# Attention and a gated network on one core: another table of pages and banks for the same work

## The chip, the core and the metric

The kernel runs on one NeuronCore of a Trainium2 chip. Its engines are named as in the profile: PE multiplies matrices (PEld loads its weights), DVE, ACT and POOL work on vectors, SP issues nearly all transfers (DMAs). The metric is the device time of one execution in microseconds (us); the time of a kernel is the median of several executions.

## The reference

Attention over 8 batches and 8 heads: 32 global positions look at everything, 512 local positions look at the global ones and at a window of 32 to each side. The result goes through a normalisation and a gated network.

```python
s_g = scale * np.matmul(q_g, k_all.transpose(0, 1, 3, 2))
out_g = np.matmul(sm(s_g), v_all)
...
s_l = np.concatenate([s_lg, s_ll], axis=-1)
out_l = np.matmul(sm(s_l), np.concatenate([v_g, v_l], axis=2))
...
xn = x / rms * rms_g
g = xn @ w_gate
silu = g * (1.0 / (1.0 + np.exp(-g)))
val = xn @ w_val
return (silu * val @ w_out)
```

There are 4608 tokens of 512 features, and 1536 hidden features.

## The kernel before

The tokens are worked through in chunks: chunks 0 to 7 are the 512 local positions of one batch each, chunk 8 holds the global positions of all. A step has a name of a chunk, a colon, a letter with numbers and a count. In a chunk, `P` are the matrix products of the network, `R` what ACT, DVE and POOL do with their results (`R45.0` computes the tanh `t11`), `t` the tail of a gated product, `w` loads and stores. `L`, `S`, `T`, `A`, `B`, `Y` and others are the attention of the next chunk, laid between them: loads of queries and keys, scores, transposes, products with values. Weights for later chunks are brought to a form of two float16 pieces once, stored to memory (`wd`, `wa`, `wb`) and loaded again as `wt` (input side) and `wu` (output side).

Nothing is scheduled by a planner at run time or by priorities: the table `ORDER` names the steps in one written order, which sets the order on every engine and in SP's queue. An instruction starts when its engine has come to it and the data and the memory that it uses are free.

All larger temporaries lie in 43 pages of 1024 float32 per partition (1152 for the 8 pages called wide, `W0` to `W7` or `w0` to `w7`), and products in 8 banks. Two more tables say where: `PAGES` has one entry for each temporary in the order in which they are asked for (1198; `13a` is page 13 from its first quarter, `41c` page 41 from its third), `BANKS` one for each product (438). `tile_of` and `bank_of` read the next entry. A temporary that is given a page waits until the last reader of the one before is done; where that reader is a transfer, until it has landed.

Some pages are neighbours in memory, in chains given by `CHAINS`; `link` holds each pair of neighbours as one piece of 2048 (two times 1024). `convert(i)` brings weight tile i (0 to 11 are `w_in`, 12 to 17 `w_out`) to its form. `load` asks for two pages; if they are neighbours, the steps behind it (rebias `m`, third piece `k`, sign `g`) work on both halves in one 1024-wide instruction, otherwise in two 512-wide ones.

Names that come up below: `t11` of step `1:R45.0`, `po2` of `1:P60.0`, `p0_11` read by `1:R45` and `1:R46`, `wq6` read by the store `1:w23.0`; `t4` of `2:R20.0`, `o1` read by the store `1:R59.1`; the loads `gv10` (`2:GL/1+1.0`), `q60` to `k61` (`1:L/0+2.0`), `wt3_21` (`3:w6.0`), `wt2_13` (`1:w49.1`), `wt2_40` (`2:w18.0`) and the temporary `s6_0` (chunk 2).

Of the kernel before, what the change touches and what calls it, by code (L numbers as in the profile page):

```python
# [62 lines left out]
NPAGE, NWIDE = 43, 8  # L63

CHAINS = (
    (7, 8, 22, 25), (9, 10), (12, 11, 18), (13, 40), (14, 4, 27, 23, 39), (15, 26), (16, 17),
    (28, 29), (30, 31), (32, 33), (34, 35), (41, 42),
)

ORDER = """  # L70
# [324 lines left out]
"""  # L395

PAGES = """
0a 0c 1a 0c 1a 5a 6a 0c 1a 11a 12a 13a 4a 2a 3a 1c 14a 15a 2a 5a 2c 4a 11a 2c 5c 7a 8a 3a 16a 17a
18a 19a 2a 20a 21a 6a 22a 8a 1a 2a 9a 10a 6a 1a 11a 18a 17a 16a 21a 1c 12a 9a 24a 1a 20a 7a 13a 0c
5c 6c 6d 0d 5d 20a 15a 23a 20b 3a 11a 10a 23a 27a 14a 4a 2a 22a 25a 28a 29a W7a 3a 11c 14a 8a 17c  # L400
27a 32a 34a 18a 19a 20c 19a 1a 6a 30a 31a 3a 7a 26a 15a 13a 40a 16a 1c 42a 34a 35a 22a 38a 2a 28a
15a 26a W2a 15c 14a 30a 41a 42a 7a 41a 7a 25a 4a 9c 38a 32a 33a 18a 29a 41c 4a 27a 23a 39a 5a 4c 24a
20c 31a 17a 33a 4c 4c 40a 4c 42a 2c 3a 9c 6a 18a 28a 11a 41c 27a 1a 9a 33a 0c 20a 18a 7a 40a 33a 36a
37a 38a W0a W1a 17a 24a 0a 2a 2a 28c 28c W3a W4a W5a W4c W6a 23a 39a 31a 3c 27a 31c 3a 0a 36a 31d 3b
2a 2b 13a 31a 31b 27c w6 w4 42a 15a 27a 2c 37c 24a 24a 41c 28a 34a 24c 41a 9a 9a 33a 27a w1 w0 5a
36a 37c 37c 13a 18a 2c 12a w0 32a 37a 23a 23a 18a 23c 21a 7a 15a 4a 19a 17c 8a 3c W6a 41c 39a 8a 36a
w2 w5 34a 17a 34c 37a 23c 3c 42a 33a 21a 27a 18a 23a 8a 4a 13a 32a 41a W7a 34a 21a 10a 0a 26a 0a 15a
22a 0a 34c 28a W5a 27c 34c 23a w7 w6 10a 13a 25a 39a 41a 39a 12c 25a 39c 41c 30a 41c 25b 37d 29a 37a
12d 37c 25c 24a 24b 23c 12a 18a 30a 13a w1 w4 35a 8a 15a 39c 4a 17a 9a 13c 41a 25c 18a 0a w4 26a W7a
19a 16a 32a 2a 22a W2a 13a 27a 3a 5a 3c 33a 19a 16a 37a 28c 21a 8a 26a 41a 0a 17a 34a 22a 5a W6a 3a  # L410
9a W0a 28a w2 w6 41c 8c 14a 28a 13a 27a 33a 2a 17a 8a 21a 5a 34a 4a 39a 13a 41c W7a 39a 3a 9a W5a
12a 36a 3a W1a 18a 33a 8a 37a 30a 21a 0a 41a 35a 34a 14a 5a 9a 32a 35a 12a 33a 41c 29a 13a 8c 29a 9a
w6 w1 13c 10a 13c 13a 14c 29a 41a 13a 22b 13c 14a 11c 17a 11a 22c 22d 29c 20a 41a 22a 13d 34a 14c
14d 4a 13a 26a 30a 31a 32a 14a w6 w2 3a 29a 0a 9a 39a 34a 37a 33a 36a 4a 42a w2 15a 40a 14a 34a 7a
31a 9a 25a 8a 28a 8c 21a 3a 15a 9a 35a 10a 42a 31a 37a 0a 11a 31c 31a 39a 34a 26a W7a 31a 36a w2 w7
34a 38a 7a 28a 21a 24a 25a 25c 1a 31c 8a 24a 12a 8a 13a 25a 19a 11a 1a 5a 7c 39c 38a 30a 26a 24a 41a
38a 10a W1a 33a 22a 27a 29c W6a 40c 35a 22c 13a 37a 5a 27a 10a 12a 26a 15a 35a 13a 24a 34a 35c 30a
3a 23a 5c 39c w2 w1 35a 18a 5a 29a 39a 4a 37a 14c 41a 5a 22a 22b W2a 5c 22c 34a 26a 23a W5a 38a 38d
29c 34a 23a 5c 38b 22c 9a 6a 38c 14c 42a 41a 24a W0a 16a 10a 42a w7 w6 40a 2a 6a 42c 26a 4a 15a 17a
32a 3a w1 8a 30c 42c 42a 29a 5a 16a 7a 14a 21a 30a 1a 39a 4a 21a 2a 39a 5a 1c 24a 16a 20a 4a 16a 37a  # L420
17a 4a W2a 14a 29a w1 w2 7a 6a 42a 26a 2a 19a 17c 17a 9a 1a 16a 20a 36a 17a 14a 9a 37a 15a 23a 25a
30a 30c 30a 31a 3a 7a 1a 37a 25a 5a 36a 31a W7a 24a 3a 24c W1a 42a 22a 0a 30a 6a 32a 39a 20a 4a 7a
30a 9a 40a 7c 1a 39a 35a 14c 7a w0 w5 7a W6a 7c 36a 14a W0a 24a 7a 12a 20c 12a 12b 19a 20c 7c 3a 35a
14a 13a 12d 30a 20a 10a W5a 7a 30c 30d 39a W4a 12c 30b 28a 23a W6a 26a 25a 32a 26a w7 w4 37a 8a 20a
15c 3a 40a 6a 28a 7a 15a w6 41a 13a 26c 20a 33a 25a 4a 1a 13c 29a 24a 21a 36a 17a 39a 25a 18a 4a 15a
20a 21a 16a 15a 26c 42a 40a 8a 31a 15a 29a w6 w5 33a 5a 24a 2a 23a W5a 1c 1a 38a 26c 28a 16a W7a 14a
3a 42a W0a 8a 33a 0a 13c 28c 28a W1a 4a 5a 9a 38a 13a 27a 26a 17a 22a 3c W4a 25a 31a 4a 4c 18a 20a
16a 37a 0a 34a 24a 30c 5a 36a 40a 12a 4a 22a W2a 3a 12a w2 w0 12c 35a 3a 15a 12a 0a 18a 34c 10a 22a
14c 14d 19a 34a 22c 25a 40a 8a 8a 14a 14b 3c 39a W2a 29a 15a 22c 24a 28a 15b 22d 4a 10a 26a W6a 41a
41a 3c w0 w1 9a 42a 12a 19a 28a 19a 4a 35a 29a 33a w1 20a 15c 12a 12c 34a 3a 37a 23a 22a 5a 38a 24a  # L430
25a 35a 12a 42a 2a 35a 19a 28a 33a 0a 3a 15c 26a 9a 37a 40a 3a 34a w3 w7 9a 21a 15c 20a 23a 18a 19c
37a 7a 38a 24a 0a 16a 3a 22a 26a 27a 18a 21a W7a 38c 3a 19c 6a 40a 24a 1a 20a 4a W2a 16a 6a W4a 15c
19c W0a 7a 0a 31a 24a 19c 25a 14a 11a 19a 35a 0a 42a 7c 7a 19c 28a 33a 7a W3a 9a 13a 33c 33a 33b 30a
30c 19a 42a 20a W7a 30c 25a 6a W1a 33c 30a 30b 35a 10a 30d 25b 32a 13a 15a W4a 36a 5a w1 w6 29a 19a
10a 31a 32a 40a 15a 14a w6 19c 19a 37a 34a 17c 36a 7a 22a 19a 31a 27a 5a 13a 2a 10a 24a 36a 36c 24a
41a 14a 17a 36a 17c 37a 21a 7a 14a W4a w2 w0 39a 22a 22c 27a 2a 34a 26a 22a 38a 8a 41a 21a W5a w6
42a 33c 24c 17a 9a 7a 12a 2a W4a 27a W3a 32a 23a 41a 20a 38a 12a 33a 12a W5a 32a 23a 23a 12a 2a W0a
15a 24a 40a 33a 17a 4a 17a 1a 6a 23c 23a 23a 15a 3a 23a 16a 33a 32a 14a 25a W6a 39a 24a 34a W5a 14a
21c 21d 11a 18a 14c 31a 8a 13a 6a W7a 20a 20b 28a 16a 20c 14c 14d 0a 21a 21b 37a 18a 30a 39a 0a 8a
9a 31a 26a 39a 28c 32a 29a 37a 7a 25a 32a W3a 30a 34a 5a 28a 20c 3a 10a 28a 27a 28a 3a W2a 24a 39a  # L440
2a 39c 14a 37a 36a 0a 42a 18a 11a 23a 9a 0a 19a 21c 29a 7a 1a 22a 29a 35a 26a 5a 23a W1a 14a 29c 38a
13a 27a 40a 27a 10a 41a 2a 12a 4a 13c 13a 15a 13a 42a 17a 31a 16a 40a
"""

BANKS = """
# [9 lines left out]
"""  # L455


# [1915 lines left out]
```

## Time and profile before

| | us |
|---|---|
| median of 3 runs | 900.91 (900.81 to 901.15) |
| profiled execution | 902.12 |
| its span, first to last instruction | 900.3 |
| PE busy | 867.6 (96%) |
| DVE busy | 709.8 (79%) |
| ACT busy | 556.1 (62%) |
| POOL busy | 278.1 (31%) |
| mean granted clock of PE | 0.989 |

The rows come from one profiled execution, 1.2 us above the median. Times in the rows count from the start of the span. Nearly every instruction is issued by one helper, so the rows have one line, L2132; they are told apart by time, tile and shape. In them `chain` is a page of a chain, `page` a single page, `wide` a wide one, `bank` a product.

### The profile page before, as it was taken

The page shows a single profiled execution, that of the slowest core. Times are in us where ns is not written, and L with a number is a line of the kernel's source. Part 1 is how long each engine was busy: PE and PEld are TensorE (multiplying, and loading weights), DVE is VectorE, ACT ScalarE, POOL GpSimd, SP SyncE. Part 2 cuts the span into 40 slices and gives each one's busy share as a digit, 9 for nine tenths or more (in the row PEclk, how much of TensorE's full clock was granted, in tenths as well). Part 3 has the DMA queues.
Part 4 walks back from the last instruction along what each step waited for, and adds up shares of the span by engine and source line. Part 5 has one row for each costly group of instructions (what it writes and reads, how often), then busy time and mean ns, then how long its engine had stood idle before and what let it go on. Part 6 is the DMA issues. An engine that isn't in the chain of part 4 may idle for free. (4 is left out here: it accounts for less than half of the span.)

```text
span 900.3 us, 28280 instructions
## 1 busy us (share of the span) xinstructions
PE 867.6 (96%) x11646; PEld 669.2 (74%) x11646; DVE 709.8 (79%) x1822; ACT 556.1 (62%) x1337; POOL 278.1 (31%) x255
## 2 busy tenths in 40 slices
PE   4799999999799899999999999999999999999998
PEld 3655456454448786588888888888888888888997
DVE  5999999888485666867876799788886888587576
ACT  6999993646334563647574775658575773545443
POOL 0000000125624467403641245214440345134414
PEclk9799999999899999999999999999999999999999
DMA  9997300688957676994799277777697579736571
GB/s 353 404 388 313 126 1 2 187 282 283 373 190 222 202 242 218 317 325 149 257 337 331 97 244 250 269 260 264 208 389 268 188 235 354 260 106 207 215 268 48
DMA packets 102737, 216.79 MB, mean 241 GB/s; under 512 B 8272, under 2 KB 34640, under 8 KB 102608
## 3 DMA queue, kind: packets, MB, share of 16 engines
q1 hardware_dynamic: 102176, 214.66, 68.8%
q8 instruction: 91, 1.49, 0.7%
q10 hardware_dynamic: 432, 0.33, 0.1%
q14 instruction: 38, 0.31, 0.1%
HBM read 187.96 MB, written 27.00 MB: 239 GB/s over the span
## 5 line engine op out<-in xcount | busy, mean ns | idle before, releaser
L2132 PEld LDWEIGHTS <-chain 128*128 128x128 f16 (+1 forms) x3744 | 346.3, 98 | 128.4 <-issue 12.9
L2132 PE MATMUL bank<-chain,chain 128*128 128x256 f16 (+6 forms) x3061 | 298.4, 270 | 5.0 <-ACT chain L2132 3.6
L2132 PE MATMUL bank<-page,chain 64*32 64x128 f32 (+5 forms) x1857 | 222.9, 298 | 1.2 <-ACT chain L2132 0.4
L2132 PEld LDWEIGHTS <-page 128*128 128x128 f16 x1704 | 160.7, 98 | 47.5 <-issue 7.8
L2132 POOL TENSOR_TENSOR chain<-chain,chain 128x512 f16<-128x512 f32 (+4 forms) x95 | 104.8, 1113 | 168.3 <-ACT chain L2132 128.3
L2132 PE MATMUL bank<-chain,page 128*128 128x256 f16 (+7 forms) x1377 | 151.8, 273 | 0.1
L2132 PE MATMUL bank<-page,page 64*32 64x128 f32 (+6 forms) x1231 | 105.0, 293 | 16.1 <-DMA page<-in_qk_dram 5.9
L2132 ACT COPY chain<-bank 128x512 f32<-128x512 f32 (+3 forms) x125 | 64.1, 531 | 79.2 <-PE bank L2132 66.5
L2132 DVE TENSOR_TENSOR chain<-bank,chain 128x512 f32<-128x512 f32 (+1 forms) x106 | 67.4, 645 | 48.5 <-PE bank L2132 32.6
L2132 ACT CAST chain<-chain 128x512 f16<-128x512 f32 (+2 forms) x87 | 66.5, 776 | 46.9 <-DVE chain L2132 36.7
L2132 ACT ACTIVATE chain<-chain,sm 128x128 f32<-128x128 f32 x200 | 74.2, 391 | 23.4 <-DVE sm L2132 23.0
L2132 POOL TENSOR_TENSOR page<-chain,page 128x512 f16<-128x512 f32 (+1 forms) x45 | 49.4, 1109 | 73.0 <-ACT page L2132 52.9
L2132 PE MATMUL bank<-wide,chain 32*64 32x96 f32 (+6 forms) x1834 | 65.5, 264 | 0.7 <-issue 0.7
L2132 ACT COPY page<-bank 128x512 f32<-128x512 f32 (+3 forms) x64 | 32.7, 519 | 44.0 <-PE bank L2132 38.8
L2132 DVE TENSOR_TENSOR chain<-chain,chain 128x256 f32<-128x256 f32 (+5 forms) x91 | 56.3, 628 | 4.6 <-ACT chain L2132 3.7
L2132 PEld LDWEIGHTS <-wide 128*128 128x128 f16 x570 | 52.9, 99 | 9.3 <-DMA wb<-chain 0.2
L2132 ACT ACTIVATE page<-page,sm 128x128 f32<-128x128 f32 x152 | 56.0, 391 | 4.4 <-DVE sm L2132 4.1
L2132 POOL TENSOR_TENSOR chain<-page,chain 128x512 f16<-128x512 f32 (+3 forms) x33 | 37.6, 1144 | 68.1 <-ACT chain L2132 64.3
L2132 POOL TENSOR_TENSOR page<-page,sm 128x512 f32<-128x512 f32 x3 | 4.1, 1368 | 176.2 <-DVE sm L2132 176.2
L2132 ACT ACTIVATE chain<-chain 128x512 f32<-128x512 f32 (+3 forms) x39 | 49.7, 1294 | 2.6 <-DVE chain L2132 1.5
L2132 PE MATMUL bank<-chain,wide 128*128 128x256 f16 (+1 forms) x392 | 48.6, 271 | 0.0
L2132 DVE CUSTOM_DVE_ANT_0 chain<-bank,wide 128x128 f32<-128x128 f32 x136 | 34.8, 283 | 12.5 <-PE bank L2132 10.1
(229 smaller groups left out, 1316.5 us busy)
## 6 DMA issues: line engine op xcount, KB each, us to landing
chain<-wd SPq DMA_DIRECT2D x77, 512.0 KB, 7.3
page<-wd SPq DMA_DIRECT2D x33, 512.0 KB, 7.6
chain<-in_w_in_dram SPq DMA_DIRECT2D x24, 512.0 KB, 9.0
chain<-wb SPq DMA_DIRECT2D x19, 512.0 KB, 7.7
wide<-in_gkq_dram SPq DMA_DIRECT2D x16, 576.0 KB, 6.6
wide<-wd SPq DMA_DIRECT2D x16, 512.0 KB, 7.9
chain<-wa SPq DMA_DIRECT2D x14, 512.0 KB, 6.6
chain<-in_vb_dram SPq DMA_DIRECT2D x18, 352.0 KB, 5.7
```

Of the source, the lines that this page charges most:

```text
L2132: return lambda *a, **k: write(self.engine, lambda: call(*a, **k))
```

## The change

The three tables are replaced: other chains, 1150 of the 1198 entries of `PAGES`, and 387 of the 438 of `BANKS`. `ORDER`, the number of pages and banks, and all code stay. The loads that asked for neighbouring pages find other neighbours: before, the two pages of all eighteen weight tiles were neighbours, now of sixteen.

```diff
 CHAINS = (
-    (7, 8, 22, 25), (9, 10), (12, 11, 18), (13, 40), (14, 4, 27, 23, 39), (15, 26), (16, 17),
-    (28, 29), (30, 31), (32, 33), (34, 35), (41, 42),
+    (1, 21), (2, 3), (6, 22), (8, 27, 30, 15, 14, 11, 12), (9, 35), (16, 17), (25, 26, 28),
+    (31, 32), (33, 34), (40, 41),
 )
...
 PAGES = """
-0a 0c 1a 0c 1a 5a 6a 0c 1a 11a 12a 13a 4a 2a 3a 1c 14a 15a 2a 5a 2c 4a 11a 2c 5c 7a 8a 3a 16a 17a
...
+0a 0c 1a 2a 2c 7a 8a 2c 9c 16a 17a 6a 10a 3a 4a 3c 18a 19a 5a 10a 5c 6a 7a 9a 7c 11a 12a 13a 20a 21a
...
 BANKS = """
-0 1 6 7 5 1 2 3 4 5 7 6 2 0 2 3 2 7 5 3 4 3 0 2 5 0 2 0 4 7 2 7 6 4 5 3 0 2 3 7 3 6 7 1 6 1 3 2 6 0
...
+0 1 6 7 1 5 2 3 4 1 7 2 6 0 2 3 2 7 3 3 4 1 0 6 4 0 6 0 3 7 6 7 2 3 4 1 0 1 1 7 6 2 7 5 0 5 2 1 3 6
...
```

The entries of the temporaries named above, read off by counting:

| temporary | before | after |
|---|---|---|
| `t11` of `1:R45.0` | 13a | 34c |
| `wq6` (store `1:w23.0`) | 13a | 18a |
| `p0_11`, `po2` | bank 4, bank 4 | bank 3, bank 7 |
| `t4` of `2:R20.0` | 41c | 15a |
| `o1` (store `1:R59.1`) | 41c | 38c |

## Rows read from the trace of the kernel before

**Rows 1.** The page's first part: busy time, share and instructions of each engine.

```profile
PE 867.6 (96%) x11646; PEld 669.2 (74%) x11646; DVE 709.8 (79%) x1822; ACT 556.1 (62%) x1337; POOL 278.1 (31%) x255
```

**Rows 2.** The waits of PE: who was waited for, total us, times, longest.

```profile
PE bank L2132 <- ACT chain L2132: 8.7, 5, 4.7
...
PE bank L2132 <- DVE chain L2132: 5.7, 5, 4.5
```

**Rows 3.** PE's timeline: start, us, operation; idle time before it and its releaser in brackets.

```profile
103.01 0.59 PE L2132 MATMUL bank<-page,chain 128*128 128x512 f16 x2 [0.27 <-DVE chain L2132]
...
111.80 0.81 PE L2132 MATMUL bank<-page,chain 128*128 128x512 f16 x3 [0.43 <-ACT chain L2132]
...
241.99 2.72 PE L2132 MATMUL bank<-page,page 128*128 128x512 f16 x6 [4.53 <-DVE chain L2132]
244.64 0.44 PE L2132 MATMUL bank<-wide,chain 64*32 64x128 f32 x4
...
295.90 1.36 PE L2132 MATMUL bank<-chain,wide 128*128 128x256 f16 x11
...
313.88 0.27 PE L2132 MATMUL bank<-chain,chain 128*128 128x256 f16 x1 [2.87 <-ACT chain L2132]
```

**Rows 4.** ACT's timeline at the two stalls.

```profile
234.49 0.35 ACT L2132 COPY page<-bank 128x256 f32<-128x256 f32 x1
...
240.53 0.69 ACT L2132 ACTIVATE chain<-bank,half_inv 128x512 f32<-128x512 f32 x1 [5.02 <-DMA wd<-chain]
...
312.64 0.72 ACT L2132 ACTIVATE chain<-page,half_inv 128x512 f32<-128x512 f32 x1 [3.56 <-DMA out_dram<-chain]
313.27 0.57 ACT L2132 COPY chain<-bank 128x512 f32<-128x512 f32 x1
```

**Rows 5.** DVE's timeline at the first stall.

```profile
241.25 0.69 DVE L2132 SCALAR_TENSOR_TENSOR chain<-chain,bank 128x512 f32<-128x512 f32 x1 [7.06 <-ACT chain L2132]
```

**Rows 6.** SP's timeline: when transfers were issued; a merged row includes waits between.

```profile
204.02 11.69 SPq L2132 DMA_DIRECT2D wd<-chain  x3
...
224.58 0.33 SPq L2132 DMA_DIRECT2D page<-in_qkb_dram  x1
...
278.38 1.25 SPq L2132 DMA_DIRECT2D wide<-wd  x2
...
284.10 0.37 SPq L2132 DMA_DIRECT2D chain<-wd  x1
...
304.77 0.46 SPq L2132 DMA_DIRECT2D out_dram<-chain  x1
```

**Rows 7.** Narrow windows: length, busy us of five engines, PE's clock, DMA share, GB/s.

```profile
242.00:246.70 4.70, 4.70 (x86) 2.77 (x93) 2.91 (x4) 0.62 (x1) 2.45 (x2) 0.50 1.05 382
...
315.00:318.40 3.40, 3.40 (x19) 2.42 (x17) 1.58 (x3) 2.75 (x11) 1.79 (x2) 0.50 1.11 379
440.00:450.00 10.00, 8.80 (x325) 7.45 (x322) 7.98 (x21) 6.07 (x9) 4.93 (x5) 1.00 0.99 385
```

**Rows 8.** Groups by shape: count, busy us, mean ns of one, idle before.

```profile
L2132 ACT CAST chain<-chain 128x1024 f16<-128x1024 f32 x34 | 35.2, 1041 | 21.1 <-DVE chain L2132 12.1 <-DVE sm L2132 5.8 <-issue 2.7
L2132 ACT CAST chain<-chain 128x512 f16<-128x512 f32 x51 | 30.7, 614 | 16.5 <-DVE chain L2132 15.4 <-PE bank L2132 0.7 <-DMA out_dram<-chain 0.2
...
L2132 DVE SCALAR_TENSOR_TENSOR chain<-chain,chain 128x512 f32<-128x512 f32 x38 | 29.2, 779 | 8.8 <-ACT chain L2132 8.8
...
L2132 DVE SCALAR_TENSOR_TENSOR chain<-chain,bank 128x512 f32<-128x512 f32 x18 | 12.1, 679 | 7.5 <-ACT chain L2132 7.5
...
L2132 DVE SCALAR_TENSOR_TENSOR chain<-chain,ends,chain 128x1024 int32<-128x1024 int32 x8 | 10.2, 1274 | 1.1 <-ACT chain L2132 1.0
```

**Rows 9.** The window of the conversions, columns as in group 7.

```profile
75.00:100.00 25.00, 24.98 (x206) 12.21 (x204) 24.71 (x56) 24.97 (x40) 0.00 (x0) 1.00 0.45 168
```

**Rows 10.** The page's DMA issues: count, KB each, median us from issue to landing.

```profile
wide<-wd SPq DMA_DIRECT2D x16, 512.0 KB, 7.9
...
chain<-in_qkb_dram SPq DMA_DIRECT2D x15, 256.0 KB, 8.3
```

More of the change, by code (lines that the diff above doesn't have):

```diff
@@ L397 @@
 PAGES = """
-0a 0c 1a 0c 1a 5a 6a 0c 1a 11a 12a 13a 4a 2a 3a 1c 14a 15a 2a 5a 2c 4a 11a 2c 5c 7a 8a 3a 16a 17a
[L399 to L442, printed above, removed]
+0a 0c 1a 2a 2c 7a 8a 2c 9c 16a 17a 6a 10a 3a 4a 3c 18a 19a 5a 10a 5c 6a 7a 9a 7c 11a 12a 13a 20a 21a
@@ new lines @@
+22a 1a 2c 23a 24a 3a 25a 26a 5a 2c 14a 15a 7a 12a 14a 11a 2a 3a 19a 18a 17a 12a 29a 18a 16a 4a 10a
+16c 23a 24c 24d 16d 23b 23c 9c 28a 23d 7a 14a 13a 15a 30a 8a 27a 20a 21a 1a 31a 32a W7a W1a 14c 4a
+25a 18c 27a W2a 26a 11a 5a 12c 5a 2a 16a 33a 34a 36a 8a 6a 22a 42a W0a 3a 2c 30a 26a 28a 31a 24a 20a
+10a 22a 6a 21a 22c 4a 33a W1a W2a 8a 35a 8a 1a 9a 0c 39a 35a 9a 11a 32a 24a 27a 30a 40a 41a 24a 9c
+29a 12c 34a 18a 36a 9c 9c 35c 9c 30a 20c 36a 0c 16a 11a 10a 39a 12c 27a 2a 12a 14a 35c 21a 11a 8a
@@ new lines @@
+23a 14a 37a 38a 24a 15a 7a 18a 29a 35a 37a 20a 10c 10c W3a W4a W5a W4c W6a 40a 41a 34a 35c 37a 34c
+35a 7a 20a 34d 35b 34a 34b 42c 27a 27b 37c w6 w4 30a 22a 29c 27c 38a 15a 36a 38c 10a 15a 29a 42a 7a
+12a 14a 36a w2 w1 0a 20a 36a 38a 18a W1a 27c 30a w1 26a 36c 36a 19a 5a 19c 40a 22a 28a 9a 29a 17a
+25a 17c W6a 38c 41a 25a 14a w7 w5 12a 37a 35c 36a 12c 17c 42c 11a 13a 38a 13a 9a 6a W0a 34c 17a 12a
+25a 19c 26a 10a 14a 40a 15a W7a 26a 14a 12c 8a W0a 34a 37c 28c w5 w6 11a 31a 38a 28c 37c 18a 30c 38a
@@ new lines @@
+28c 38c 35a 38c 38b 32d 13a 32a 30d 32c 19c 18c 18d 20a 30a 31a 35a 36a w2 w4 29a 41a 40a 1c 4a 0a
+10a 30a 37c 30a W5a 17a w2 11a 4a 3a 19a W6a 27a 26a W1a 36a 1a 37a 22a 28a 33a 22a 10a 32a 28a 25a
+17a 11a 37c 15a 0a 34a 26a 10a 41a 5a 22a 5a 18a w2 w1 15a 15c 7a 18a 4a 6a W2a 27a 0a 37a 35a 6a
+25a 8a 1a 38c 15a W7a 6a 17a 27a 34a 19c 19a 17a W4a 33a 35a 32a 1c 5a 8a W0a 37c 3a 11a 25a 38a 7a
+35a 3a 27a 6a 18a 35a 18c 30c 7a 17a w0 w6 7c 9a 7a 18c 16a 18a 38a 16c 26d 7a 11a 26a 0a 18c 16c
@@ new lines @@
+16d 7c 21a 37c 26c 16a 25a 26a 26b 14a 23a 29a 19a 12a 1a 12c w0 w1 27a 40a 30a 17a 25c 37a 1a 6a
+15a 14a 42a w1 W2a 40c 7c 17a 31a 37a 12a 34a 10a 32a 10c 20a 27a 42a 15a 24a 25a 42a 7c 30a 38a 13a
+12a 7c W7a 33a 23a 3a 37a 2a w7 w4 33a 18a 37c 31a 20a W4a 32c 25a 19a 12a 10a 13a 8a 19a 37a 30a
+28a 6a 13a 5a 32a 32c 25a 11a 23a 18a 9a 18a 10a 14a 3a 16a 41a W6a W0a W6c W1a 40c 16c 34a 7a 27a
+42a 8a 23a 12a 26c 28a W4a 37a 23a 11a 33a 17a 25a 26a w7 w6 23c 29a 40c 26c 25a 24a 34a 7a W6a 13c
@@ new lines @@
+13a 13b W7a 26a 28a 8a 37a 21a 35a 18a 18d 7c 8a 21a 1a 18b 28a 34a 39a 18c 28c 32a 24a 3a 36a 22a
+39a 26a w0 w1 30a 4a 40a 15a 37a 33a 1a 0a 25a 15a w6 35a 26c 26a 13c 19a 22a 32a W2a 11a 20a 11c
+16a W2a 40a 16a 36a 40a 22a 28b 3a 19a 10a 33a 15c W4a 0a 20a W7a 26c 32a w0 w4 34a 12a 26a 37a 20a
+9a 10a 15c W0a 11c 19a 0a 2a 10a 11a 36a W7a 1a 21a 41a 13c 13a 13c 5a 33a 11a 22a 13a 41a 35a 2a 5a
+W1a W7a W0a W7c W4a 26a 15c 38a 33a 12a 25a 40a 0a 11a 3a 33a 36a 30a 15a 3a 40a 29a 26a 15c w6 w7
@@ new lines @@
+15c 4a 15a 36a 38a W6a 26a 15c 14a 15a 36c 36d 9a 8c 36a 0a 3a 27a 7a 8d 38a 8a 39a 27a 38c 8a 8b
+40a W5a 8c 38b 31a 21a W0a 29a 20a 25a 38c w1 w5 33a 34a 15a 34c 0a W4a 15a 31a 12a 19a w0 7a 32a
+29a 36a 6a 11a 20a 1a 32c 24a 3a 16a 13a 10a 29a 11a 23a 21a 34a 0a 3a 2a 34a 36a 28a 19a 40a W7a
+34a 9a w7 w6 6a 35a 32c 24a 31a W6a 23a 16c 18a 36a 20a 1a W5a 27a 16a 28a W1a 2a 6a 30a 14a 35a 16c
+4a 33a 20a 41a 7a 14a 42a 32a 10a 22a 23c 40a W4a 11a 36a 38c W0a 33a 21a 35a 20a 37a 30a 8a 36a 13a
@@ new lines @@
+19a 38c 4a 22a W2a 23a 33a w6 w2 38a 26a 33a 34a 23a 39a 11a 37c W6a 6a 27c 27d 5a 37a 6c 40a 19a 2a
+2a 27a 27b 33c 29a W2a 9a 34a 6c 16a 16a 34b 6d 4a 10a 32a W0a 18a 18a 16a w1 w5 W7a W1a 23a 34c 25a
+28a 4a 26a 9a 39a w5 8a 34c 6a 21a 36a 33a 35a 31a 7a W6a 7c W2a 21a 28a 23a 25a 24a 26a 16c 37a 33a
+5a 6a 8a 32a 40a 35a 19a 6a 36a w3 w6 40a 3a 16c 8a 31a 11a 26a 5c 12a W2a 7a W6a W0a 0a 26c 32a 20a
+35a 3a 0a 5a 26a 5c 15a 19a 11a 1a 26a 4a 2a 16a 15a 42a 27c 6a W1a 12a 8a 38a 11a 6a 21a 27a 17a
@@ new lines @@
+42a 28a 6a 25a 42c 6c 42c 37a 33a 8a W0a 40a 14a 15c 15a 15b 41a 41c 42a 35a 0a W3a 41c 21a 33a 38a
+15c 41a 41b 28a 7a 41d 21b 30a 14a 29a W6a 13a 39a w7 w5 9a 42a 38a 12a 13a W2a 11a 27a w5 42a 15c
+10a W7a 29a 30a 8a 1a 14a 12a 5a 39a 42a 24a 38a 24a 15c 30a 26a 7a 27a 22a 8a 9a 10a 3a 28a 27a W2a
+w1 w7 2a 15c 24a 5a 1a 29a 32a 26a 20a 19a 7a 3a W4a w5 35a 21c 15c 24c 40a 28a 4a 1a W2a W4a W0a
+13a 31a 7a 0a 20a 4a 24c 4a 15a 13a 31a 2a 19a 1a W1a 11a 24a 30a 21a 9c 23a 9a 34a 33a 21a 21c 21c
@@ L443 @@
+11a 36a 21c 16a 2a 31a 27a 4a W5a 13a 34a 29a W7a 27c 27a 27b 17a 25a 27a 39a 28a 42a 24a W6a 0a 0b
+37a 16a 0c 3c 27c 6a 3a 3b 5a 37a 41a 8a 6a 31a 40a 39a 10a 34a 29a 31a 15a 5a 32a 14a 25a W0a 41a
+37a 12a 28c 0c 33a 38a 25a 14a 5a 13a 22a 4a 42a 1a 8a 28a 26a 20a 29a 35a 8a 10a 11a 40a 29a 21a
+27a 12c 17a 36a 34a 33a 18a 28a 41a 19a W3a 12a 15a 23a 32a 33a W1a 15a 6a W4a 1a 11a 7a 12a 12c 30a
+35a 12a 9a 39a 32a 13a
 """
 BANKS = """
[9 rows of a table removed]
[9 rows of a table added]
 """
```

16 rows, old and new, of the table BANKS are left out of this document.

## Prediction

> **What bounds the kernel now.** I read the page's busy table first: PE is busy 867.6 us of a span of 900.3, 96% [rows 1], so only PE's idle time and its clock can give anything back; a faster engine beside it gives nothing. The list of what PE waited for comes second [rows 2]: 8.7 us for ACT in five waits, the longest 4.7, and 5.7 us for DVE in five, the longest 4.5. The reader is to see that this is a handful of stalls, not many small ones. PE's timeline then places them. Those of the first 50 us follow loads and data, which the change leaves alone. Two lie later: 4.53 us before 241.99, behind DVE, and 2.87 us before 313.88, behind ACT [rows 3].
>
> The third reading is what held those engines. ACT's timeline shows, at 240.53, an activation that had waited 5.02 us for a DMA that reads a page into `wd`, and at 312.64 one that had waited 3.56 us for a DMA into the output [rows 4]. DVE's instruction at 241.25 waited 7.06 us for the first of these [rows 5], and PE for DVE. So the causes of both PE stalls are pages: a temporary was given a page that a slow store was still reading. By the tables, `t11` (step `1:R45.0`) shares page 13 with `wq6`, which store `1:w23.0` reads; the product `po2` (step `1:P60.0`) shares bank 4 with `p0_11`, which waits to be read by `R45` and `R46`. `t4` (step `2:R20.0`) shares page 41 with `o1`, which store `1:R59.1` reads. The second store was issued at 304.77 [rows 6], 7.9 us before its ACT instruction began, which is about as long as a transfer takes here [rows 10]; the first lies in the same way.
>
> The fourth reading is the clock. [...] Behind two short idle times within 440 to 450 us it stays 1.00 [rows 7]. [...]
>
> **The change part by part.** No operation, no DMA and no order is altered, only the page and the bank of each temporary.
>
> *First stall.* In the new tables `t11` has page 34, which no store reads late, and `po2` has bank 7, which ACT empties with the copies that end at 234.84 [rows 4]. ACT had been idle since 240.53 - 5.02 = 235.51 [rows 4] with its input there, and PE's work before the stall ended at 241.99 - 4.53 = 237.46 [rows 3]. `P60` needs neither `R45` nor `R46` for its data, so it follows at once: 4.53 us. Half of the 4.70 us at the half clock [rows 7] goes too, since the same columns take half the time: 2.35 us. Together 6.9 us. What is late next is a chain over POOL and DVE whose result PE wants some 8 us later; followed step by step on the old times it moves with PE but for some 0.2 us, so I keep 6.7.
>
> *Second stall.* `t4` moves to page 15, which DVE has released by then. ACT, idle since 312.64 - 3.56 = 309.08, runs `t4` there (0.72), and the copy that PE waits for (0.57) follows by 310.4 [rows 4]; PE's earlier work ends at 313.88 - 2.87 = 311.01 [rows 3]. The cover is 0.6 us. Gain 2.87 + 3.40/2 = 4.57 us. What is late next is weight tile `wt2_40`, issued right behind the store of 304.77 [rows 6] and first used 4 us behind the stall, some 4.2 us after its landing; the gain eats that margin, and I put 0.2 us against it: 4.4 kept.
>
> *Small bank waits.* One of 0.27 us at 103.01 [rows 3] and one more of 0.2 come from a shared bank that is no longer shared; I count 0.3 as gain. The 0.43 us at 111.80 [rows 3] are data and stay.
>
> *What is added, first: split conversions.* A weight whose two halves lie on neighbouring pages of one chain is converted in 1024-wide instructions. By the tables all eighteen were so before; now tiles 12 and 14 (`w_out` 0 and 2) are not. "Sixteen joined" is thus two fewer, and costs six instructions: two on ACT, four on DVE. ACT: 2 x 0.614 - 1.041 = 0.19 us each; DVE: 2 x 0.679 - 1.274 = 0.08, or 2 x 0.779 - 1.274 = 0.28, each [rows 8]. That makes 0.37 us on ACT and 0.3 to 1.1 on DVE. They run between 85 and 115 us, where ACT is busy 24.97 and DVE 24.71 of 25 us [rows 9], so no cover is there but PE's own lead; PE has three short waits behind these engines. Ends 0 and 1.5; I take 0.4, nearest to the ACT row, since the wait at 111.80 is behind ACT. [...]
>
> *What is added, second: holds of the DMA queue.* SP issues all these transfers in the written order; one whose page is not yet free holds all behind it. The new tables let freed pages rest longer before ACT, DVE or POOL reuse them (least time between a store's landing and a compute instruction on its page: 5.5 us instead of under 0.1), and pay with loads that take pages sooner. I laid the new pages on the old times. The worst hold is 12.2 us (`gv10`, from 202.9), in a stretch where the queue stood 11.7 us inside three stores anyway [rows 6]. What hangs on it is loads up to that at 224.58 [rows 6], some 2 to 3 us later, so from 226.6, landing 8.3 us after issue [rows 10] at 234.9; they are first used at 244.64 [rows 3], 238.8 once the stall is gone: 3.9 us left. The next: the load issued at 278.38 is held until `s6_0` is released at 284.10, as the next load was before [rows 6]; plus 7.9 us [rows 10] is 292.0, against first use at 295.90 [rows 3]: 3.9 left. Three more, at 287, 518 and 716 us, keep 5 to 6.5. Every load still lands in time: cost 0, with ends 0 and some 14 (the slower rival). PE's start may lose 0.3 by an ACT instruction there that now shares a page with a later reader, and the end of the program 0.1.
>
> *The sum*, against the profiled execution's own 902.12 us: 902.12 - 6.7 - 4.4 - 0.3 + 0.4 + 0.3 + 0.1 = 891.5. The median of the runs shown is 1.2 us below the profiled execution, so the median to come is 890.3.
>
> **The rivals.**
> (a) Half of it is kept. The chain POOL, DVE, PE behind 250 us, or a load, takes the first stall's place; then 6.7 us stay lost: 897.0. Or the second stays: 894.7. For it: DVE waits for POOL at several places between 245 and 265. Against it: POOL's work there follows results of PE and ACT that move too.
> (b) The change does not do what it says: both waits find another late reader, and the time stays at 901. Against it: the new pages of `t11` and `t4` were free 4 us and more before these two began, by the tables on the old times.
> (c) Slower: the holds of SP's queue outgrow the margins. Transfers pile up behind a hold and start together when it ends, so each could land later than its row says. If five places with 3.9, 3.9, 4.7, 5.9 and 6.5 us left are each held 7.0 us more, PE loses 3.1 + 3.1 + 2.3 + 1.1 + 0.5 = 10.1, and behind the two longest the half clock costs 2.35 + 1.70 again [rows 7]: 14.2 us, so 904.5. The point from which it decides is about 6.3 us more at each, where some 6.7 + 4.05 eat the whole gain of 10.6. Against it: 7.0 us is nearly a whole transfer's 7.9 [rows 10].
> (d) The clock. The new banks could make PE pause shortly and often, and the clock fall between: each fall at the price of rows 7, about 2 us; one or two of these give 892 to 894.5. The short pauses of the old run left it at 1.00 [rows 7]. [...]
>
> **How the numbers follow.** Forecast 0.70; (a) 0.14; (b) 0.05; (c) 0.08; (d) 0.03. The forecast's own range is 888.5 (splits free, no follower) to 892 (splits at their upper end, wt2_40 late). The range to hold 8 in 10 goes on through (d) and (a) to 897.5, and a little below for slack that I do not see: 887.5 to 897.5. Faster by over 0.2% (1.8 us, about what a measurement of this kernel can tell from no change): 0.70 + 0.14 + 0.02 and no more, 0.86; within 0.2%: 0.06; slower: 0.08.
>
> **What would show it.** Right, if in the new profile PE has no stall over 1 us after 50 us, the clock is 1.00 from 225 to 320, and ACT's waits for `wd<-chain` and `out_dram<-chain` are gone; the splits show as six more instructions between 85 and 115, and PE's waits there grow by under 1 us. Wrong in (a): a new PE wait near 238 or 250, or 311. Wrong in (c): PE or its weight loads wait for a DMA `chain<-wd` or `chain<-in_qkb`, above all near 239, 290, 297, 525 and 725, with SP waiting just before. What would make the whole wrong is a transfer that lands far later than its row of the old run, since all margins are laid on old times.

## The result and the profile after

| | before | after |
|---|---|---|
| median, us | 900.86 (900.05 to 901.15, 4 runs) | 889.75 (888.94 to 890.10, 4 runs) |
| profiled execution, its span | 902.12, 900.3 | 889.73, 887.9 |
| PE busy, mean granted clock | 867.6, 0.989 | 862.6, 0.991 |

The ratio is 0.9877, 95% interval 0.986 to 0.9894: 11.1 us faster by the medians, and 12.4 us between the two profiled executions (902.12 and 889.73). The forecast said 890.3.

The list of PE's waits after the change (who was waited for, total us, times, longest us), against [rows 2]:

```profile
PE bank L2133 <- DMA chain<-in_qk_dram: 5.7, 1, 5.7
PE bank L2133 <- DVE chain L2133: 5.3, 3, 4.9
PE bank L2133 <- ACT chain L2133: 5.0, 1, 5.0
PE bank L2133 <- ACT page L2133: 1.8, 3, 1.2
...
PE bank L2133 <- DVE sm L2133: 0.8, 1, 0.8
```

Three long waits are left, 5.7, 4.9 and 5.0, all in the first 40 us. The 4.53 and the 2.87 us of [rows 3] are gone, and a wait of 0.8 behind DVE's `sm` is new. The windows of the two stalls and of the short pauses (length, busy us of PE, PEld, DVE, ACT, POOL, granted clock, DMA share, GB/s), against [rows 7]:

```profile
225.00:250.00 25.00, 24.96 (x458) 13.59 (x457) 17.97 (x59) 10.07 (x28) 16.33 (x13) 1.00 1.06 370
300.00:325.00 25.00, 25.00 (x293) 21.61 (x292) 21.42 (x56) 19.62 (x58) 16.10 (x12) 1.00 0.85 293
440.00:450.00 10.00, 10.00 (x92) 8.72 (x91) 7.27 (x20) 5.20 (x12) 5.92 (x6) 1.00 1.01 318
```

PE is busy for all but 0.04 us of the 25 us in each of the first two, and the granted clock is 1.00. In the timelines (start, us, operation, idle time in brackets) the places of [rows 3] and [rows 4] now read, first PE's:

```profile
237.99 1.70 PE L2133 MATMUL bank<-chain,chain 128*128 128x512 f16 x10
...
304.60 1.47 PE L2133 MATMUL bank<-chain,chain 128*128 128x256 f16 x12
```

ACT's timeline of the same kernel:

```profile
236.13 0.67 ACT L2133 ACTIVATE chain<-bank,half_inv 128x512 f32<-128x512 f32 x1
...
302.66 0.72 ACT L2133 ACTIVATE chain<-page,half_inv 128x512 f32<-128x512 f32 x1
303.54 0.59 ACT L2133 COPY chain<-bank 128x512 f32<-128x512 f32 x1 [0.16 <-PE bank L2133]
```

`P60`, at 237.99, and `P25`, which now runs within the row at 304.60, follow the work before them without a pause; `t11` (236.13) and `t4` (302.66) begin as soon as ACT comes to them.

Lining up every product of PE in the two traces gives the time by place: the start of the same product, after minus before (a negative number is time gained by then).

| at (us, before) | after minus before, us | what lies between |
|---|---|---|
| 43 | +0.79 | start |
| 213 | -0.18 | conversions, short bank waits |
| 236 | +0.69 | the new wait of 0.83 before `1:P30.0` |
| 250 | -6.26 | first stall and its slow clock: -6.95 |
| 300 | -6.25 | |
| 320 | -10.95 | second stall and its slow clock: -4.70 |
| 450 | -11.91 | short waits |
| 890 | -12.38 | short waits |

### The profile page after: what moved, and what is told of

Its sections match the earlier page's. It is cut to its first block, busy times and chain, and to the rows that moved or that the text cites. A ratio compares the mean times of both kernels' runs of the same rounds, so it can differ in the third digit from the quotient of the medians.

```text
span 887.9 us, 28263 instructions
## 1 busy us (share of the span) xinstructions
PE 862.6 (97%) x11646; PEld 666.8 (75%) x11646; DVE 710.8 (80%) x1826; ACT 555.6 (63%) x1339; POOL 279.1 (31%) x255
## 4 chain that ended last, share of the span: by engine, by line
PE 84%; DVE 5%; ACT 2%; issue 1%; DMA 1%; POOL 0%; SPq 0%; POOLq 0%; ACTq 0%
PE bank L2133 84%; DVE chain L2133 3%; DVE page L2133 2%; ACT chain L2133 1%; DMA wide<-in_gkq_dram 1%; ACT page L2133 1%; DVE wide L2133 0%; POOL chain L2133 0%; SPq L2133 0%; POOL page L2133 0%; DVE nt L2133 0%; DVE xg L2133 0%; DVE sm L2133 0%; DVE hs L2133 0%; ACT sm L2133 0%
## 5 line engine op out<-in xcount | busy, mean ns | idle before, releaser
L2133 PEld LDWEIGHTS <-chain 128*128 128x128 f16 (+1 forms) x3369 | 309.9, 98 | 105.2 <-issue 7.8
L2133 PE MATMUL bank<-chain,chain 128*128 128x256 f16 (+5 forms) x2406 | 263.0, 277 | 1.7 <-DVE sm L2133 0.8
L2133 PE MATMUL bank<-page,chain 128*128 128x256 f16 (+6 forms) x1689 | 203.3, 289 | 0.9 <-DMA page<-in_qk_dram 0.6
L2133 PE MATMUL bank<-chain,page 128*128 128x256 f16 (+6 forms) x1887 | 181.9, 286 | 11.9 <-DMA chain<-in_qk_dram 5.7
L2133 PE MATMUL bank<-page,page 128*128 128x256 f16 (+5 forms) x1171 | 119.7, 277 | 1.7 <-ACT page L2133 1.4
L2133 POOL TENSOR_TENSOR chain<-chain,chain 128x512 f16<-128x512 f32 (+5 forms) x66 | 73.8, 1125 | 131.8 <-ACT chain L2133 95.4
L2133 POOL TENSOR_TENSOR page<-chain,page 128x512 f16<-128x512 f32 (+3 forms) x50 | 56.8, 1147 | 97.5 <-ACT page L2133 97.3
L2133 PE MATMUL bank<-chain,wide 128*128 128x256 f16 (+3 forms) x482 | 61.5, 278 | 0.1
L2133 ACT COPY page<-bank 128x512 f32<-128x512 f32 (+2 forms) x73 | 38.3, 541 | 35.5 <-PE bank L2133 31.8
L2133 ACT CAST page<-chain 128x512 f16<-128x512 f32 (+2 forms) x42 | 33.9, 813 | 34.9 <-DVE chain L2133 28.2
L2133 POOL TENSOR_TENSOR chain<-page,chain 128x512 f16<-128x512 f32 (+3 forms) x34 | 38.9, 1150 | 52.5 <-ACT chain L2133 52.5
```

The costliest lines, as they stand in the source:

```text
L2133: return lambda *a, **k: write(self.engine, lambda: call(*a, **k))
```

## The experiments

The kernel before and the changed kernel were run again beside them; before had medians of 899.5 to 900.6 and the changed kernel 889.58 (888.15 to 890.27). Each run is compared by its ratio to the kernel before on its own chip; the ratios stand with their 95% intervals in brackets and are not exactly the quotients of the medians. Entries of a table are counted from 0.

> The changed kernel itself, beside the next two on one chip: 889.7 by every theory.

It measured 889.58, ratio 0.9883 (0.9864 to 0.9901).

### One entry: t11

Entry 263 of `PAGES`, the third of these five:

```diff
-8a 4a 13a 32a 41a
+8a 4a 16c 32a 41a
```

> The kernel before with one entry of the page table changed: t11 of step 1:R45.0 goes from page 13 (still read by the store of wq6) to the third quarter of page 16, which nobody has used for long. Theory (one shared page is the whole first stall): PE's wait of 4.53 us before 1:P60.0 and the half clock behind it go, 6.7 to 7.1 us, so 893.8 to 894.2. Rival (the next wait in the chain over POOL and DVE takes its place): 1 to 4 us gained, 897 to 900. Rival (the wait belongs to the bank that po2 shares, so the page alone does nothing): 900.9.

Measured: 903.83 against 899.51, ratio 1.0037 (1.0019 to 1.0056): slower. PE's row of this run:

```profile
251.05 0.61 PE L2132 MATMUL bank<-nt,same 128*128 128x16 f32 x2 [7.12 <-DVE sm L2132]
```

DVE's row:

```profile
249.47 0.29 DVE L2132 CUSTOM_DVE_ANT_0 chain<-bank,wide 128x128 f32<-128x128 f32 x1 [6.76 <-DMA wd<-chain]
```

Two of its windows, columns as above:

```profile
246.00:251.00 5.00, 0.00 (x0) 0.00 (x0) 1.45 (x13) 0.39 (x2) 0.00 (x0) 0.68 1.08 381
251.00:255.00 4.00, 3.95 (x12) 1.73 (x13) 3.74 (x17) 1.50 (x9) 0.00 (x0) 0.54 1.06 355
```

The same place in the kernel before, first DVE's rows:

```profile
248.68 0.29 DVE L2132 CUSTOM_DVE_ANT_0 chain<-bank,wide 128x128 f32<-128x128 f32 x1 [1.67 <-DMA wd<-chain]
...
249.22 0.29 DVE L2132 CUSTOM_DVE_ANT_0 chain<-bank,wide 128x128 f32<-128x128 f32 x1 [0.24 <-DMA wd<-chain]
```

And PE's row there, with no wait before it:

```profile
250.42 0.39 PE L2132 MATMUL bank<-nt,same 128*128 128x16 f32 x2
```

The wait before `P60` is gone, PE comes to `1:n55.0` 6.5 us earlier (251.05 - 7.12 = 243.93, against 250.42), and waits there 7.12 us. What holds it is DVE at 249.47: `e600` is written to a page that the store `1:w51.0` reads, and that store lands only 0.8 us later than in the kernel before, although PE is 6.5 us earlier. In the kernel before, DVE waited for stores there too, until 248.68 and 249.22, and it cost nothing more, because PE, late from its first stall and slow behind it, came to `n55` at 250.42 just as DVE was done. So that point is set by the stores with or without the first stall. All of the gain is given back there; and where the slow clock of the kernel before ran ahead of this point, it now comes behind it (0.54 in the 4 us from 251) and adds, as an estimate, some 1.8 us (0.46 of 4). All three expectations fell; the second was right in kind and wrong in size.

### One entry: t4

Entry 359 of `PAGES`, the second of these three:

```diff
-w6 41c 8c
+w6 24c 8c
```

> The kernel before with one entry changed: t4 of step 2:R20.0 goes from page 41 (still read by an output store) to the third quarter of page 24. Theory: PE's wait of 2.87 us before 2:P25.0 and the half clock behind it go, 4.4 to 4.6 us, so 896.4. Rival (the weight tile wt2_40 then lands late, since its margin of 4.2 us is used up): 2 to 4 us gained, 897 to 899.

Measured: 897.90 against 899.51, ratio 0.9979 (0.9965 to 0.9992): faster, by 0.7 to 3.2 us. In its profile PE's wait before `P25` is gone and PE, lined up with the kernel before, gains 4.7 us between 310 and 320, as expected, and `wt2_40` is in time; two waits grew by 0.5 us each near 440 to 450. The timed runs give less than the profile, and the kernel before ranged from 896.7 to 902.3 on that chip, so how much of the 4.7 us an ordinary execution holds is not settled by this run alone.

### Both entries

`t11` and `t4`:

```diff
-13a 41c
+16c 24c
```

> The kernel before with both entries changed, t11 and t4, and the other 1196 pages, the banks and the chains as they were. Theory (two entries of some 1500 are the whole change): 6.8 + 4.5 us gained, 889.6, within 1.5 us of the changed kernel. Rival (the longer rest of all the other pages and banks carries a good part): 893 or more.

Measured: 900.71 against 899.51, ratio 1.0013 (1.0001 to 1.0025). The rival is right, and by more than it said: two entries together give nothing. Against the run with `t11` alone (1.0037) the second entry does gain, some 2 us; the loss at the first stall's follower takes it up. PE's row at the same place as above:

```profile
251.74 0.61 PE L2132 MATMUL bank<-nt,same 128*128 128x16 f32 x2 [7.01 <-DVE sm L2132]
```

### The new banks with the old pages

The whole table of banks of the changed kernel:

```diff
 BANKS = """
-0 1 6 7 5 1 2 3 4 5 7 6
+0 1 6 7 1 5 2 3 4 1 7 2
...
```

> The kernel before with the changed kernel's table of banks and its own pages. Theory (page and bank are links of one chain): 1:P60.0 no longer waits for the bank of p0_11, but t11 is still late, and the score product s610 of 1:S/0+2.0, which now has that bank, waits in its place until about 242; PE keeps a wait of some 3 us there and the half clock behind it, the second stall stays, and some short bank waits go: 897.5 to 899.5. Rival (taking the bank away is as good as taking the page away): 6.8 us and some 0.7 of short waits, 893.4.

Measured: 902.55 against 899.51, ratio 1.0026 (1.0006 to 1.0046). PE's row of this run:

```profile
244.57 0.44 PE L2132 MATMUL bank<-wide,chain 64*32 64x128 f32 x4 [4.02 <-DVE chain L2132]
```

ACT's row:

```profile
242.33 0.69 ACT L2132 ACTIVATE chain<-bank,half_inv 128x512 f32<-128x512 f32 x1 [5.02 <-DMA wd<-chain]
```

`P60` runs in time, and PE waits 4.02 us a little later, before the first score product that needs the bank behind `t11`; ACT still waits 5.02 us for the store. The theory has the place right; its sum was 3 to 5 us too low, since the wait was 4 us and not 3, the clock falls behind it as well (0.51 in the 5.4 us from 244.6), and PE had come there 1.8 us late, 1.6 of it from the first 45 us. The bank alone is worth nothing: the wait goes to the next owner of the bank.

### The stretch: seven entries

`t11`, `t4`, `e600`, `e611`, `wq11`, `y2` and `h2_3`, in the order of the lines below; banks and chains stay the old ones, and `t11` has another free page than in the runs above:

```diff
-13a 41c 25a 25c 10a 39a 39a
+W2c 24c 7a 16c W5a W2c 7c
```

> The kernel before with seven entries changed: t11 and t4 as in the runs before it, and the five temporaries that come behind t11 and share a page with stores of the same stretch: e600 and e611 (read by store 1:w51.0 until 249.1 in the kernel before), wq11 (1:w51.0), y2 and h2_3 (1:w35.0, until 255.9). The run with t11 alone showed PE's wait moved from 1:P60.0 to 1:n55.0, 7.1 us, behind e600. Theory (one wait stands behind another because SP's stores land when the queue gets to them, whatever PE does; the gain comes when all of a stretch are gone): 11 us gained, 888.5 to 890. Rival (still another page takes over, one that the two traces do not show as late): 892 to 898.

Measured: 891.58 against 900.64, ratio 0.9895 (0.9874 to 0.9916): 9.5 us. Between this kernel and the one with two entries lie five more entries and some 10 us. Two windows of this run:

```profile
225.00:250.00 25.00, 24.30 (x456) 13.35 (x456) 17.15 (x55) 9.78 (x26) 14.81 (x13) 1.00 1.06 372
...
300.00:325.00 25.00, 24.85 (x291) 21.34 (x289) 21.05 (x55) 19.34 (x58) 15.42 (x12) 1.00 0.90 299
```

PE's row at `1:n55.0`:

```profile
244.54 0.39 PE L2132 MATMUL bank<-nt,same 128*128 128x16 f32 x2 [0.70 <-DVE sm L2132]
```

The clock stays at 1.00, and of the 7 us at `n55` a wait of 0.70 is left. Seven entries carry nearly all of the change, with the old banks; the intervals of the two ratios overlap, so how much the other 1143 pages and the banks add, some 1 to 1.6 us by the ratios, is not certain.

### The wait put back into the changed kernel

Entry 263 of `PAGES`, `t11`, in the changed kernel's table:

```diff
-34c
+18a
```

> The changed kernel with t11 of step 1:R45.0 put back onto the page of wq6 (18 in its table), whose store lands at 244.7 there, 4.2 us later than in the kernel before, because SP's queue runs later. The banks stay those of the changed kernel. Theory: t11 waits until 244.7, 1:P60.0 runs in time, and the product s610, which has the bank that t11 is made from, waits until about 246: a wait of PE of 6 to 7 us near 240 to 246, and the half clock behind it, 2.3 to 3.3 us: 898 to 900. Rival (the stall was a matter of the bank alone, which stays apart for po2): 889.7.

Measured: 897.49, ratio 0.9974 (0.9963 to 0.9984), by the ratios some 8 us over the changed kernel; half a microsecond under the lower end expected. The wait is as long as expected; the slow clock behind it cost less, some 1.5 us (0.39 of 3.8). PE's row:

```profile
246.20 0.44 PE L2133 MATMUL bank<-chain,chain 64*32 64x128 f32 x4 [6.54 <-DVE page L2133]
```

ACT's row:

```profile
243.95 0.69 ACT L2133 ACTIVATE page<-bank,half_inv 128x512 f32<-128x512 f32 x1 [7.50 <-DMA wd<-page]
```

The window behind the stall:

```profile
246.20:250.00 3.80, 3.80 (x131) 3.37 (x132) 2.84 (x10) 0.60 (x1) 2.46 (x2) 0.61 1.06 381
```

One shared page makes a wait of 6.54 us and a stretch at 0.61 of the clock. So a single entry can lose what a single entry could not win, and the banks, which stay the new ones here, do not save it.

### A longer hold of the queue, within and past the margin

In `fetch`, first `wt2_02` once more, then, in another kernel, `wt3_20` itself once more:

```diff
+        if (c, g, i) == (3, 2, 0):
+            o, d, n = 3, 3, 2
+            nc.sync.dma_start(chunks[2]["wt"][0, 2][:, :n], wd[0][:, o : o + d * (n - 1) + 1 : d])
...
+        if (c, g, i) == (3, 2, 0):
+            nc.sync.dma_start(t[:, :n], wd[g][:, o : o + d * (n - 1) + 1 : d])
```

> The changed kernel with one more transfer in SP's queue, at step 3:w4.0: weight tile wt2_02 is loaded a second time onto its own page, and so must wait until its first load has landed, at 227.8. What is queued behind it, the loads q60, k60, q61 and k61, comes some 2.8 us later. In the changed kernel the last of them lands at 236.3 and is first used at 239.5, 3.2 us later. Theory (the hold is hidden while it is shorter than that margin): 889.7, PE without a wait near 239. Rival (every hold of the queue is paid): 892 to 893.

Measured: 888.92, ratio 0.9877 (0.9862 to 0.9892), as the changed kernel.

> The changed kernel with one more transfer at step 3:w4.0, but of weight tile wt3_20 itself, which lands only at 230.3: the loads behind it come 5 to 5.5 us later, past their margin of 3.2 us. Theory (the margin is the point from which a hold costs): PE waits 1.8 to 2.5 us near 239 and pays up to 2 us more if its clock falls behind that: 891.5 to 894. Rival (the queue catches up, since transfers take only as long as they do because many run at once): 889.7.

Measured: 892.15, ratio 0.9911 (0.9896 to 0.9926), 3.2 us over the run above, on the same chip. SP's row when `q60` and `k60` are issued, in the changed kernel:

```profile
225.90 1.03 SPq L2133 DMA_DIRECT2D chain<-in_qkb_dram  x2
```

The same with the hold within the margin:

```profile
227.73 1.74 SPq L2136 DMA_DIRECT2D chain<-in_qkb_dram  x2
```

And past it, with the row that holds the queue:

```profile
221.34 8.43 SPq L2135 DMA_DIRECT2D page<-wd  x2
...
230.77 1.52 SPq L2135 DMA_DIRECT2D chain<-in_qkb_dram  x2
```

PE's rows in the last, where the loads are used:

```profile
239.06 0.42 PE L2135 MATMUL bank<-chain,chain 64*32 64x128 f32 x8 [0.86 <-DMA chain<-in_qkb_dram]
240.77 0.31 PE L2135 MATMUL bank<-chain,page 64*32 64x128 f32 x4 [1.29 <-DMA chain<-in_qkb_dram]
```

The window of these waits:

```profile
239.00:243.00 4.00, 2.65 (x130) 2.13 (x131) 3.04 (x8) 0.00 (x0) 3.39 (x3) 1.00 1.10 378
```

The loads go out 1.8 us later in the first of the two and 4.9 us later in the second. The first costs nothing, the second two waits of 0.86 and 1.29 us, behind which the clock stayed at 1.00. The two profiled executions differ by 2.5 us (spans of 886.4 and 888.9), and these waits are 2.15 of it; that of the second kernel is the fastest of its four, and where the rest of the 3.2 us between the medians lies is open. One wait of 1.05 us near 432, for a load of `in_vb`, stands in the second trace; the last run of this document has it too, with 1.44 us and without a hold, so it need not come from the hold. A hold is thus free at 1.8 us and paid at 4.9: this fits the margin of 3.2 us in the changed kernel's trace and does not fix the point. The rival of the second run is right in part, since the queue catches up a little: `q60` landed 7.5 us after its issue in the changed kernel and 6.1 and 5.7 us after it in these two. Times to landing of one kind differ with the load in the kernel before too: two stores of 256 KB to the output landed 2.0 us after issue (median) between 870 and 900 us, where the DMA share is 0.14, and two between 330 and 360 us, where it is 0.73, 7.1 us after.

### All weight tiles split

```diff
-            both = link.get(tuple(at[::-1] if turned else at))
+            both = None
```

> The changed kernel with the remaining sixteen weight tiles split too: each conversion in 512-wide pieces, 48 more instructions, 19 on ACT and 29 on DVE. By the rows of the kernel before, 0.19 us each on ACT and 0.08 to 0.28 on DVE, 3.6 and 2.3 to 8.1 us, part of it beside idle time. Theory (the step of the forecast, 0.2 us for each tile): 3.2 us, 893. Rival (PE's lead and the idle time hide it): under 0.8 us, 889.7 to 890.5. [...]

In this kernel the two halves of the tiles that were loaded in turned order end up exchanged, which changes values but no instruction's size. Measured: 889.37, ratio 0.9883 (0.9869 to 0.9898): nothing that the interval can tell, for 48 instructions; the rival is right. The first part of the page, of the changed kernel:

```profile
PE 862.6 (97%) x11646; PEld 666.8 (75%) x11646; DVE 710.8 (80%) x1826; ACT 555.6 (63%) x1339; POOL 279.1 (31%) x255
```

One of its groups by shape (count, busy us, mean ns of one):

```profile
L2133 ACT ACTIVATE chain<-chain 128x1024 int16<-128x1024 int16 x10 | 24.8, 2506 | 0.1
```

The first part of the page with all tiles split:

```profile
PE 863.0 (97%) x11646; PEld 667.4 (75%) x11646; DVE 712.4 (80%) x1855; ACT 555.6 (63%) x1358; POOL 279.3 (31%) x255
```

And the same group there:

```profile
L2133 ACT ACTIVATE chain<-chain 128x512 int16<-128x512 int16 x20 | 24.8, 1383 | 0.0
```

ACT has 19 more instructions and the same 555.6 us of busy time; DVE has 29 more and 1.6 us, 0.055 each. Ten instructions of 2.506 us became twenty of 1.383, and both groups are busy for 24.8 us: two that follow each other overlap, and the sum of their durations counts the overlap twice. One pair with all tiles split, in ACT's timeline, takes 2.50 us together, as long as one undivided:

```profile
59.52 2.50 ACT L2133 ACTIVATE chain<-chain 128x512 int16<-128x512 int16 x2
```

The kernel before shows the overlap as well, in ACT's timeline:

```profile
229.55 0.62 ACT L2132 CAST page<-page 128x512 f16<-128x512 f32 x1
230.07 0.61 ACT L2132 CAST wide<-chain 128x512 f16<-128x512 f32 x1
230.59 0.61 ACT L2132 CAST chain<-chain 128x512 f16<-128x512 f32 x1
```

Each lasts 0.61 to 0.62 us and the next starts 0.52 us after it, an overlap of 0.09 to 0.10; in the `int16` pair it is larger, some 0.27 us (2 x 1.383 - 2.50). By the rows of single instructions the expectation had 3.6 us on ACT and 2.3 to 8.1 us on DVE; the busy time grew by none and by 1.6.

### The new wait of 0.83 us

PE's row in the changed kernel:

```profile
214.77 1.45 PE L2133 MATMUL bank<-chain,chain 128*128 128x512 f16 x6 [0.83 <-DVE sm L2133]
```

DVE's row there:

```profile
210.09 1.26 DVE L2133 TENSOR_TENSOR page<-page,chain 128x256 f32<-128x256 f32 x1
```

POOL's row there:

```profile
208.62 2.45 POOL L2133 TENSOR_TENSOR page<-chain 128x512 f32<-128x512 f16 x2 [1.33 <-PE bank L2133]
```

The same operation of DVE in the kernel before:

```profile
210.21 0.42 DVE L2132 TENSOR_TENSOR page<-page,chain 128x256 f32<-128x256 f32 x1
```

And POOL's there:

```profile
207.62 2.27 POOL L2132 TENSOR_TENSOR wide<-page 128x512 f32<-128x512 f16 x2
```

In the changed kernel POOL waits 1.33 us for the page of `os2`, which PE still reads as `k50`; its two operations then run until 211.07, across an operation of DVE that takes 1.26 us where it took 0.42 with POOL done at 209.89. DVE ends 0.28 us after POOL; why its operation is longer beside POOL's, no run shows. DVE is then late with `s500`, and `P30` needs its bank.

The banks of `s500` and `s510` exchanged:

```diff
-1 4
+4 1
```

> The changed kernel with the banks of two score products exchanged, s500 (1 to 4) and s510 (4 to 1). In the changed kernel PE has one new wait of 0.83 us at 214.8: 1:P30.0 needs bank 1, which DVE reads for s500 until 214.7, and DVE is late there because one 256-wide operation took 1.26 us instead of 0.42 while POOL was at work. Theory (the wait is the bank's): the wait goes, 0.6 to 0.8 us, 889.0. Rival (DVE's lateness reaches PE by the data too): unchanged, 889.7.

Measured: 889.18 (888.79 to 889.35), ratio 0.9882 (0.9865 to 0.9899). PE's row:

```profile
213.64 2.54 PE L2133 MATMUL bank<-chain,chain 128*128 128x512 f16 x11
```

DVE's row:

```profile
209.96 1.26 DVE L2133 TENSOR_TENSOR page<-page,chain 128x256 f32<-128x256 f32 x1
```

DVE is as late as before (1.26 us), and PE no longer waits: the link was the bank. By the medians it is 0.4 us, which the intervals cannot tell from nothing.

With these banks, the page of `sq0` moved too:

```diff
-2c
+W7a
```

> The same with one more entry: sq0 of step 0:Q0.0 goes from page 2, which it shares with e10, to the wide page 7, free at that time. In the changed kernel Q0.0 waits there and PE waits 1.21 us at 29.6, against 0.53 before. Theory: another 0.4 to 0.7 us, 888.4, faster than both kernels. Rival (PE's wait at 29.6 follows data, not the page): as the one above, 889.0.

Measured: 888.64 (888.04 to 889.82), ratio 0.9878 (0.9859 to 0.9896). The lowest median of all, but only 0.9 us under the changed kernel, with ranges that overlap: not shown to be faster. The rival is right on `sq0`: PE's wait at 29 us is 0.91 here and was 1.21 and 0.87 in the two traces of the changed kernel and 0.35 in the run with the banks alone, so it varies from execution to execution and the page does not set it.

## Why the prediction was right

**The bound.** PE's stalls and the clock behind them were the time, as the prediction read from [rows 2] to [rows 7]: of 12.4 us between the profiles, 11.65 lie at the two stalls. The signs that it named are there: the longest wait of PE after 50 us is 0.83 us (a second trace of the same kernel has one of 1.10 at 639), the clock is 1.00 from 225 to 320, ACT no longer waits for `wd<-chain` or `out_dram<-chain`, and ACT and DVE have two and four instructions more.

**First stall.** 6.7 us were forecast, 6.95 measured. The step that took 0.2 us off for a follower behind 250 us was not needed. But as an account of the cause the step was incomplete. It named one page and one bank, and the run with that page alone gained nothing: behind it stood `e600`, held by a store that landed at nearly the same time whether PE was late or not, and not the chain over POOL and DVE that the prediction followed. The bank was not needed: the run with seven entries keeps the old banks. The forecast held because the rest of the new table moves the other pages too; the prediction had this only as one number in its paragraph on holds, the 5.5 us that a freed page now rests at least. Rival (a) put 6.7 us on such a follower: with the old pages it is there, in the changed kernel it is not.

**Second stall.** 4.4 us forecast, 4.7 measured between the two profiles; `wt2_40` took nothing. The timed runs with `t4` alone show 0.7 to 3.2 us, so that an ordinary execution loses all of the 4.7 there is not shown.

**Split conversions.** 0.4 us forecast, none measured: PE's wait at 111.80 went from 0.43 to 0.37 us. The failed step is the price: durations of single rows [rows 8] were subtracted as if instructions did not overlap, and the ACT row was that of a cast, while the two ACT instructions that were split are ACTIVATEs. Splitting the other sixteen cost nothing either. Of the three short waits that the prediction counts between 85 and 115 us the trace shows two, at 103.01 and 111.80.

**Holds of the queue.** Cost 0 was right. The margin for `q60` to `k61` was forecast at 3.9 us; the changed kernel has 3.2 (last landing 236.3, first use 239.5), and the run past it paid as rival (c) would, 3.2 us over the one within. Rival (c) feared that loads behind a hold land later than their rows; those looked at landed sooner after their issue, 6.1 and 5.7 us against 7.5 without the hold. Rival (c) needed five such places at once.

**Small terms.** The waits of 0.27 and 0.2 us are gone as forecast. Not foreseen: between 320 and 890, where other short waits lie, 1.4 us were gained in this trace of the changed kernel and 0.6 in its second, so these vary from execution to execution; and a new wait of 0.83 came at 214.8. For the new tables the prediction listed what waits for stores, and not that POOL would wait there for a page that PE reads, nor what DVE does beside POOL. The term of 0.3 us for the start is not confirmed: at 43 us two traces of the changed kernel differ by 0.98 (+0.79 and -0.19 against the kernel before).

**The clock.** Half the time of each stretch at the half clock, 0.50 [rows 7], was counted as gain, and the trace of the kernel before bears that out: from its start at 241.99 to the next row, 244.64, [rows 3] has six products of 512 columns in 2.65 us, and six of the same shape take 1.30 us from 250.66 to the next row, at 251.96, where the clock is 1.00:

```profile
250.66 1.46 PE L2132 MATMUL bank<-chain,chain 128*128 128x512 f16 x6
251.96 1.46 PE L2132 MATMUL bank<-page,chain 128*128 128x512 f16 x6
```

Rival (d) did not come: the granted clock is 1.00 in the windows shown, and also on the mean from 50 to 450 and from 450 to 880 us.

**Luck in the number.** The sum was made against a profiled execution that lay 1.2 us above its median; the new one lies at its median. The sum for the profiled execution was 891.5, and it measured 889.73: it moved 12.4 us where 10.6 were forecast. The 1.2 us taken off to come to the median made up for most of that. The medians moved 11.1 us. So the match of 890.3 with 889.75 is in part luck, two errors that cancel; that the two stalls would go, with the slow clock behind them, was read from the rows and came.

## What to carry to other kernels

A wait for a page that a store still reads can be one of a row: in the runs with `t11` alone and with both entries the stores landed only 0.8 and 1.6 us later than in the kernel before, so taking one such wait away brought the engine to the next one sooner, and the gain came only when the pages of the whole stretch were clear. So list the landings of the stores in a stretch and every temporary that shares their pages, not only the one that is waited for now. The cost of more and smaller instructions is read from the distance of their starts or from the busy sum of a group, not from the duration of one: here casts of 0.61 us on ACT started 0.52 us apart.

## What the runs showed of the hardware

In these runs the slow clock behind a stall cost time only where nothing else set the pace. In the kernel before, a clock of 0.50 in the 4.7 us behind 242 lay ahead of a point that PE could not have passed much before 250.4, because stores held DVE until 249.22; in the run with `t11` alone a slow stretch came behind that point, and the kernel was 0.4% slower. Two waits of 0.86 and 1.29 us close together left the clock at 1.00.

DVE's operation that reads two pages (128x256) took 1.26 us in the changed kernel, across one of POOL, and 0.42 in the kernel before, where POOL was done.

Two ACT instructions of 512 columns, one right behind the other, took 2.50 us together, as long as one of 1024 (2.506).
